# Relative-position attention before a dense block: the softmax reciprocals of a head pair leave for DRAM in three transfers instead of sixteen

## The chip, the core and the metric

One NeuronCore of a Trainium2 chip runs the whole kernel. The metric is the device time of one execution in microseconds (us), lower is better; a kernel's figure is the median of its timed runs. The profile is of one more execution, taken by the hardware profiler.

## What is computed

Attention for 8 batch elements, 8 heads, 576 positions and a head width of 64, with a bias that a small two-layer network makes from the distance of two positions, and then a dense block on the 4608 tokens. Cut to what matters:

```python
scores = q @ k.T / sqrt(64) + bias[h]            # 576 x 576 for each batch element and head
attn   = exp(scores - max(scores, axis=-1))
attn   = attn / (sum(attn, axis=-1) + 1e-09)     # the sums this change is about
x      = (attn @ v), heads side by side          # 4608 tokens x 512
out    = ((x @ w1) * (x @ w2)) @ w3 @ w_out
```

The kernel leaves the division for later: it stores the unnormalised product `exp(...) @ v` and, apart from it, the reciprocals of the sums, and multiplies the two when the dense block loads its tokens.

## The kernel before

**Stages.** A first stage (to about 60 us of the trace) makes the bias. Then come 32 attention units of about 12.2 us each, up to about 470 us: unit u is head pair p = u // 8 and batch element b = u % 8 (`units`). The dense block fills the rest, and TensorE (PE) is busy there without a break that matters here.

**One unit.** Nine tiles of scores (`TILES`, "0" to "7" for four row blocks of each of two heads, "M" for the last 64 rows of both heads) go through `op_S` (PE), `op_T` (VectorE, DVE: bias and row maximum), `op_E` (ScalarE, ACT: exponential, with the row sum as a by-product), `op_F` (PE transposes), `op_H` (ACT or DVE move them out of PSUM) and `op_W` (PE: times v). The steps of consecutive units overlap. On PE, ACT, DVE and GpSimd (POOL) the order is written out by hand in `ORDER`, one start time per step in a unit of `PERIOD`, and each engine executes in that order: an instruction that waits holds all behind it. The order of the DMA issues on the SP queue isn't written out; the Tile scheduler decides it. The SP queue, too, is worked off in order.

**The sums.** `sums[p]` is one tile of 128 x 72: a column for each tile of each of the eight units of a head pair. In the last unit of a pair `op_r` adds 1e-9 and takes the reciprocal (L529, L530), `op_F` "N" transposes the 72 columns, `op_H` "N" copies them to `rts[p]` (72 x 128), and `op_r` "d" writes `rts[p]` to `r_d` in DRAM, laid out head by head and there token by token (L534, L535): two DMAs for each of the eight batch elements. This happens four times, after units 7, 15, 23 and 31. The readers of `r_d` are the loads of the dense block (`load_x`, L836), which begin after unit 31.

**A piece of a weight in each unit.** The dense block's weights arrive in 8-byte form and are turned to float32 in pieces, one in most units (`pieces`; none in units 7, 8, 15, 23 and 31). The eight steps of a piece come from `narrow`: `fetch` (L322, a load of 512 KB into `wi` on the SP queue), `size` (L327, ACT), `rest` (L333, POOL), `clamp`, `shift`, `head` and `power` (DVE, `power` at L359) and `total` (L364 and L365, POOL). There is one buffer `wi` for all pieces, so a `fetch` waits until the piece before has done L364, the last step that reads it. The steps have their places in `ORDER` as "c1" to "c7"; "c1" (L327) stands between two exponentials of ACT.

**Other loads on the SP queue.** In each unit `load` issues `rq` and `rk` (L452, the unit's q and k), `rv` (L452) and `rt` (L456, the last 64 columns of q), and `op_x` stores the product (L608).

Of the kernel before, what the change touches and what calls it, by code (L numbers as in the profile page):

```python
# [13 lines left out]
AF = mybir.ActivationFunctionType  # L14
# [4 lines left out]
P = 128  # L19
# [239 lines left out]
def relpos_attention_moe(  # L259
# [17 lines left out]
    nc = tc.nc  # L277
    NPAIR, B, _, S = k.shape
# [120 lines left out]
    r_d = [r_all[:, p] for p in range(NPAIR)]  # L399
# [13 lines left out]
    NB, sums, rts = {}, {}, {}  # L413
# [5 lines left out]
    def halves(x):  # L419
        return x.rearrange("p (a j) -> p a j", a=2)  # L420
# [90 lines left out]
    def op_E(u, t):  # L511
        d = st[u]
        ts, mx = d.pop(("t", t))
        p, b = units[u]
        if p not in sums:
            sums[p] = sm.tile([P, 9 * B], F32, name="sum")
        if t == "M":
            pp, col = PM2[u % 2][:, 64:64 + S], 8
        else:
            h, i = int(t) % 2, int(t) // 2  # L520
            if ("P", i) not in d:
                d["P", i] = ppool.tile([P, 2 * S], F32, name="pp", bufs=NPP)
            pp, col = d["P", i][:, h * S:(h + 1) * S], i + 4 * h
        nc.scalar.activation(pp, ts, AF.Exp, bias=mx, scale=-1.0, accum_out=sums[p][:, 9 * b + col:9 * b + col + 1])  # L524

    def op_r(u, n):
        p, b = units[u]
        if n == "":
            nc.vector.tensor_scalar(sums[p], sums[p], 1e-9, None, op0=ALU.add)  # L529
            nc.vector.reciprocal(sums[p], sums[p])  # L530
        else:
            for c in range(B):
                rows, x = r_d[p][:, c * S:(c + 1) * S], rts[p][9 * c:9 * c + 9]
                nc.sync.dma_start(rows[:, 0:512].rearrange("h (i j) -> h i j", j=P), x[0:8])  # L534
                nc.sync.dma_start(rows[:, 512:S].rearrange("(o h) j -> o h j", o=1), x[8:9])  # L535

    def turn(ps, c0, x):
        for hf, rows in enumerate((lo, hi)):
# [80 lines left out]
    for m, u in enumerate(UP_IN):  # L619
        w = (moe_w1, moe_w2)[m].rearrange("(c p) n -> p c n", p=P)[:, :, 0:P]  # L620
        x = wu0[:, (1 - m) * DM:(2 - m) * DM]
        pieces[u] = narrow(cva, w, DM, x, nc.sync, pieces=NC, low=nc.gpsimd, both=True)

    def op_c(u, n):
        pieces[u][int(n)]()

    made = dict(l=lambda u, n: load(u, n[1]), g=op_g, S=op_S, T=op_T, E=op_E, r=op_r, F=op_F, W=op_W, x=op_x, c=op_c)
    later = []
    for (n, u), (at, on) in arrange(NU, pieces).items():
# [112 lines left out]
    PM2 = [ppool.tile([P, S + P], F32, name=f"ppM{i}") for i in range(2)]  # L742
# [556 lines left out]
    for c in range(NPR):  # L1299
# [8 lines left out]
        if c + 1 < NPR:  # L1308
            x = next(coming)
# [9 lines left out]
        if prior:  # L1319
            e, d = prior[-1], down["1"]  # L1320
# [5 lines left out]
        d = down["4"]  # L1326
# [76 lines left out]
```

## Time and profile before

| | |
|---|---|
| median of 3 runs | 1069.78 us (1069.55 to 1073.88) |
| profiled execution, its own time | 1068.68 us |
| its span (first to last instruction) | 1066.5 us |
| mean granted clock of PE | 0.988 |
| PE, DVE, ACT, POOL busy | 97%, 77%, 62%, 34% of the span |
| DMA issues `r_d<-rt` on the SP queue | 32 of 4 KB (L534), 32 of 0.5 KB (L535) |

The profiled execution lies 2.2 us over its span and 1.1 us under the median. Times of the trace count from the start of the span. "SPq" names an issue on the SP queue: its duration is how long the queue is held, not how long the data travel. A note in brackets behind an instruction is the idle time of its engine before it and what ended that. A granted clock of 1.00 is PE's upper level (2.4 GHz), 0.50 the lower (1.2 GHz).

### The profile page before, as it was taken

What the parts mean: (1) busy time and instruction counts of PE and PEld (TensorE: products, weight loads), DVE (VectorE), ACT (ScalarE), POOL (GpSimd) and SP (SyncE); (2) the same over time, 40 slices, a digit from 0 to 9 for tenths busy, and PEclk for the clock granted to TensorE, in tenths of its full rate; (3) what the DMA queues carried; (4) which work ended last, traced back from release to release, by engine and by line L of the source; (5) the groups of instructions that cost most, each with busy time, mean ns of one, the idle gap of its engine ahead of it and who ended that gap; (6) DMA issues with size and microseconds to landing.
All of it is one profiled execution on the core that took longest, in us unless ns stands there. A gap on an engine that the chain in (4) does not pass through costs nothing. (4 is left out here: it accounts for less than half of the span.)

```text
span 1066.5 us, 22676 instructions
## 1 busy us (share of the span) xinstructions
PE 1029.6 (97%) x8816; PEld 826.0 (77%) x8816; DVE 818.9 (77%) x1529; ACT 658.5 (62%) x1199; POOL 360.1 (34%) x337
## 2 busy tenths in 40 slices
PE   6979999999799979999999999999999999999998
PEld 2357777777577757767899998888888888888887
DVE  8968888888588868856988997978477757774664
ACT  8879989998599969973644553445234533453232
POOL 0067755675567656722000154611211111100100
PEclk9989999999899989999999999999999999999999
DMA  7965474547454645316569669885777577743623
GB/s 244 312 185 172 155 252 142 189 155 233 141 167 158 211 146 165 122 64 162 169 211 307 255 236 334 284 281 183 225 247 268 185 230 242 271 150 122 234 96 136
DMA packets 80331, 214.39 MB, mean 201 GB/s; under 512 B 11232, under 2 KB 29024, under 8 KB 75104
## 3 DMA queue, kind: packets, MB, share of 16 engines
q1 hardware_dynamic: 66080, 142.30, 41.1%
q0 software_dynamic: 13136, 68.98, 19.7%
q10 hardware_dynamic: 1008, 1.66, 0.5%
q8 instruction: 70, 1.15, 0.4%
q14 instruction: 37, 0.30, 0.1%
HBM read 163.06 MB, written 49.84 MB: 200 GB/s over the span
## 5 line engine op out<-in xcount | busy, mean ns | idle before, releaser
L1092 PE MATMUL b<-xu,w 128*128 128x462 f32 (+1 forms) x1728 | 366.2, 372 | 1.1 <-ACT wos L1103 0.9
L1092 PEld LDWEIGHTS b<-xu,w 128*128 128x128 f32 x1728 | 325.2, 188 | 38.7 <-ACT wos L1103 1.3
L499 DVE CUSTOM_DVE_ANT_0 ts<-s,nb 128x576 f32<-128x576 f32 x288 | 208.1, 754 | 42.3 <-ACT pp L524 16.8
L524 ACT ACTIVATE pp<-ts,mx 128x576 f32<-128x576 f32 x256 | 195.4, 766 | 4.4 <-DVE mx L499 4.4
L1092 PE MATMUL b<-xu,w3s 128*128 128x462 f32 (+1 forms) x840 | 179.6, 372 | 0.0
L1092 PEld LDWEIGHTS b<-xu,w3s 128*128 128x128 f32 x840 | 158.1, 188 | 18.0
L599 PE MATMUL pst<-pt,rv 128*64 128x256 f32 (+1 forms) x1280 | 171.9, 416 | 0.2 <-ACT pt L567 0.2
L1103 ACT COPY wos<-b 128x462 f32<-128x462 f32 (+1 forms) x151 | 81.2, 542 | 137.5 <-PE b L1092 135.6
L930 DVE TENSOR_TENSOR wos<-b,wos 128x462 f32<-128x462 f32 (+1 forms) x126 | 79.7, 637 | 111.5 <-PE b L1092 109.9
L567 ACT ACTIVATE pt<-pst 128x1024 f32<-128x1024 f32 x128 | 130.4, 1021 | 42.7 <-PE pst L540 42.1
L599 PEld LDWEIGHTS pst<-pt,rv 128*64 128x64 f32 x1280 | 87.2, 138 | 63.6 <-issue 8.1
L565 DVE COPY pt<-pst 64x64 f32<-64x64 f32 (+3 forms) x160 | 82.2, 514 | 40.0 <-PE pst L599 35.2
L540 PE MATMUL pst<-ident,pp 64*128 64x64 f32 x2304 | 95.8, 225 | 12.7 <-ACT pt L567 12.1
L540 PEld LDWEIGHTS pst<-ident,pp 64*128 64x128 f32 x2304 | 90.2, 141 | 14.0 <-ACT pt L567 12.9
L488 PE MATMUL s<-kh,qh 64*128 64x288 f32 x512 | 96.3, 367 | 4.8 <-POOL kh L470 3.1
L850 ACT ACTIVATE w<-wu 128x768 fp32r<-128x768 f32 (+1 forms) x45 | 40.4, 907 | 95.8 <-PE b L1092 73.3
L1084 POOL DMA_DIRECT2D w<-ws_d x24 | 17.3, 721 | 202.3 <-PE b L1092 186.0
L850 ACT ACTIVATE xu<-g 128x924 fp32r<-128x924 f32 (+1 forms) x60 | 55.9, 969 | 41.4 <-DVE g L930 39.7
L1278 POOL DMA_DIRECT2D w3s<-dw_d x33 | 18.0, 547 | 181.3 <-DVE w3s L853 111.7
L488 PE MATMUL s<-kh,ql 64*128 64x288 f32 x512 | 78.0, 298 | 0.6 <-DVE ql L468 0.6
L488 PE MATMUL s<-kl,qh 64*128 64x288 f32 x512 | 77.8, 297 | 0.7 <-POOL kl L471 0.7
L471 POOL TENSOR_TENSOR ql<-rq,qh 128x1024 fp32r<-128x1024 f32 x31 | 73.9, 2385 | 2.6
(118 smaller groups left out, 1464.4 us busy)
## 6 DMA issues: line engine op xcount, KB each, us to landing
w3s<-dw_d POOLq DMA_DIRECT2D x33, 1024.0 KB, 7.2
w<-ws_d POOLq DMA_DIRECT2D x24, 1024.0 KB, 5.6
rq<-in_q_dram SPq DMA_DIRECT2D x28, 512.0 KB
wi<-in_moe_w_dram SPq DMA_DIRECT2D x22, 512.0 KB
nb_d<-bev SPq DMA_DIRECT2D x36, 295.5 KB
rv<-in_v_dram SPq DMA_DIRECT2D x32, 320.0 KB
x_d<-pt SPq DMA_DIRECT2D x32, 288.0 KB
wu<-wu_d SPq DMA_DIRECT2D x24, 384.0 KB
```

The costliest lines, as they stand in the source:

```text
L471: nc.gpsimd.tensor_tensor(l, x, f(h), op=ALU.subtract)
L488: nc.tensor.matmul(s[:, hf, :HS], Q[x][rows, h * 512 + i * P:h * 512 + (i + 1) * P], K[y][rows, h * HS:(h + 1) * HS], start=(m == 0), stop ...
L499: nc.vector.tensor_tensor_reduce(out=halves(ts), in0=d.pop(("s", t))[:, :, :HS], in1=halves(NB[p, t]), op0=ALU.add, op1=ALU.min, scale=-1. ...
L524: nc.scalar.activation(pp, ts, AF.Exp, bias=mx, scale=-1.0, accum_out=sums[p][:, 9 * b + col:9 * b + col + 1])
L540: nc.tensor.transpose(ps[0:n, hf, c0:c0 + 64], x[rows], ident[rows, rows])
L565: nc.vector.tensor_copy(o, x)
L567: nc.scalar.activation(o, x, AF.Copy)
L599: nc.tensor.matmul(o, x[:, c0:c0 + D], m, start=(c == 0), stop=(c == 4))
L850: nc.scalar.activation(o, x, AF.Copy)
L930: return lambda: nc.vector.tensor_tensor(o(), a(), b(), op=op)
L1092: nc.tensor.matmul(acc, w(l), x(r), start=start and i == 0, stop=stop and i == 2, skip_group_check=True)
L1103: return h, pl.step("ACT", 0.16 + n / 1200, lambda: nc.scalar.copy(spare(h, n)(), bank(src, n)()), after, [src], [h])
```

## The change

The 72 columns of `sums[p]` get another order. Before, unit b owned columns 9b to 9b+8: four of head 0, four of head 1, one of tile M. Now head 0 has columns 0 to 31, head 1 columns 32 to 63 (4b + i within the head), and tile M of all units columns 64 to 71. After the transpose these columns are rows of `rts[p]`, so that all of a head's rows stand together in the order in which `r_d` wants them. The write to DRAM is then one DMA of 32 x 128 for each head and one of 8 x 128 for the M rows, in place of eight DMAs of 8 x 128 and eight of 1 x 128. The bytes, and the runs of 512 and 256 bytes that they are made of, are the same. The exponential, the addition, the reciprocal, the transposes and the copy keep their sizes.

```diff
--- before.py
+++ after.py
@@ -515,13 +515,13 @@
         if p not in sums:
             sums[p] = sm.tile([P, 9 * B], F32, name="sum")
         if t == "M":
-            pp, col = PM2[u % 2][:, 64:64 + S], 8
+            pp, col = PM2[u % 2][:, 64:64 + S], 8 * B + b
         else:
             h, i = int(t) % 2, int(t) // 2
             if ("P", i) not in d:
                 d["P", i] = ppool.tile([P, 2 * S], F32, name="pp", bufs=NPP)
-            pp, col = d["P", i][:, h * S:(h + 1) * S], i + 4 * h
-        nc.scalar.activation(pp, ts, AF.Exp, bias=mx, scale=-1.0, accum_out=sums[p][:, 9 * b + col:9 * b + col + 1])
+            pp, col = d["P", i][:, h * S:(h + 1) * S], 4 * (h * B + b) + i
+        nc.scalar.activation(pp, ts, AF.Exp, bias=mx, scale=-1.0, accum_out=sums[p][:, col:col + 1])
 
     def op_r(u, n):
         p, b = units[u]
@@ -529,10 +529,13 @@
             nc.vector.tensor_scalar(sums[p], sums[p], 1e-9, None, op0=ALU.add)
             nc.vector.reciprocal(sums[p], sums[p])
         else:
-            for c in range(B):
-                rows, x = r_d[p][:, c * S:(c + 1) * S], rts[p][9 * c:9 * c + 9]
-                nc.sync.dma_start(rows[:, 0:512].rearrange("h (i j) -> h i j", j=P), x[0:8])
-                nc.sync.dma_start(rows[:, 512:S].rearrange("(o h) j -> o h j", o=1), x[8:9])
+            x = rts[p]
+            rows = r_d[p].rearrange("h (c j) -> h c j", j=S)
+            for h in range(2):
+                nc.sync.dma_start(
+                    rows[h][:, 0:512].rearrange("c (i j) -> c i j", j=P), x[4 * B * h:4 * B * (h + 1)],
+                )
+            nc.sync.dma_start(rows[:, :, 512:S].rearrange("h c j -> c h j"), halves(x[8 * B:9 * B]))
 
     def turn(ps, c0, x):
         for hf, rows in enumerate((lo, hi)):
```

On PE, ACT, DVE and POOL the instructions stand in the same order as before. On the SP queue only the sixteen transfers of each head pair are replaced. `DMAHW` names one of eight counters which the DMAs of the hardware queues use in turn; a wait on one is a wait for the DMA that used it last.

The SP queue after unit 15 (head pair 1), before. Ahead stands the load of k, behind the transfers the load of the last q columns (L456), the piece of unit 17 (L322) and a later unit's q (L452):

```order
L452 DMA rk<-in_k_dram 128x576 [waits DMAHW4_49,PE_49]
L534 DMA r_d<-rt 2x4x128 [waits DMAHW5_49,DVE_49]
L535 DMA r_d<-rt 2x1x64 [waits DMAHW6_49]
...
L534 DMA r_d<-rt 2x4x128 [waits DMAHW3_49]
L535 DMA r_d<-rt 2x1x64 [waits DMAHW4_49]
L456 DMA rt<-in_q_dram 128x128 [waits DMAHW5_49]
L322 DMA wi<-in_moe_w_dram 128x1024 [waits DMAHW6_49,Activation_49,Pool_49]
L452 DMA rq<-in_q_dram 128x1024 [waits DMAHW7_49,Pool_49]
```

The same place now:

```order
L452 DMA rk<-in_k_dram 128x576 [waits DMAHW7_49,PE_49]
L535 DMA r_d<-rt 8x4x128 [waits DMAHW0_49,DVE_49]
L535 DMA r_d<-rt 8x4x128 [waits DMAHW1_49]
L538 DMA r_d<-rt 8x2x64 [waits DMAHW2_49]
L456 DMA rt<-in_q_dram 128x128 [waits DMAHW3_49]
L322 DMA wi<-in_moe_w_dram 128x1024 [waits DMAHW4_49,Activation_49,Pool_49]
L452 DMA rq<-in_q_dram 128x1024 [waits DMAHW5_49,Pool_49]
```

Thirteen issues between the load of k and the load of `rt` are gone, and the piece's load keeps its place behind `rt`; it waits as before for ACT and POOL, the readers of the piece before. Units 23 to 25 (head pair 2) read the same.

The SP queue after unit 7 (head pair 0), before; no piece stands right behind the transfers here, since the load for unit 9 was issued far ahead:

```order
L452 DMA rk<-in_k_dram 128x576 [waits DMAHW7_49,PE_49]
L534 DMA r_d<-rt 2x4x128 [waits DMAHW0_49,DVE_49]
...
L535 DMA r_d<-rt 2x1x64 [waits DMAHW7_49]
L456 DMA rt<-in_q_dram 128x128 [waits DMAHW0_49]
L452 DMA rq<-in_q_dram 128x1024 [waits DMAHW1_49,Pool_49]
L452 DMA rv<-in_v_dram 128x640 [waits DMAHW2_49,PE_49]
```

The same place now:

```order
L452 DMA rk<-in_k_dram 128x576 [waits DMAHW7_49,PE_49]
L535 DMA r_d<-rt 8x4x128 [waits DMAHW0_49,DVE_49]
L535 DMA r_d<-rt 8x4x128 [waits DMAHW1_49]
L538 DMA r_d<-rt 8x2x64 [waits DMAHW2_49]
L456 DMA rt<-in_q_dram 128x128 [waits DMAHW3_49]
L452 DMA rq<-in_q_dram 128x1024 [waits DMAHW4_49,Pool_49]
L452 DMA rv<-in_v_dram 128x640 [waits DMAHW5_49,PE_49]
```

Here, too, thirteen issues are gone, ahead of `rt`, `rq` and `rv`.

## Rows read from the trace of the kernel before

**Rows 1.** The page, part 1: busy time, share of the span, instructions of each engine

```profile
PE 1029.6 (97%) x8816; PEld 826.0 (77%) x8816; DVE 818.9 (77%) x1529; ACT 658.5 (62%) x1199; POOL 360.1 (34%) x337
```

**Rows 2.** Waits of PE, whole span: us in total, times, longest

```profile
PE pst L540 <- ACT pt L567: 12.1, 3, 6.2
```

**Rows 3.** Timeline of PE: start us, us, line, operation, [idle before it <- releaser]

```profile
183.62 0.27 PE L547 MATMUL pst<-ident,ppM 64*128 64x64 f32 x1
...
195.85 0.27 PE L547 MATMUL pst<-ident,ppM 64*128 64x64 f32 x1
...
269.61 0.27 PE L547 MATMUL pst<-ident,ppM 64*128 64x64 f32 x1
...
278.04 1.11 PE L540 MATMUL pst<-ident,pp 64*128 64x64 f32 x16 [6.18 <-ACT pt L567]
...
290.82 0.27 PE L547 MATMUL pst<-ident,ppM 64*128 64x64 f32 x1
...
376.74 0.27 PE L547 MATMUL pst<-ident,ppM 64*128 64x64 f32 x1
...
384.64 1.12 PE L540 MATMUL pst<-ident,pp 64*128 64x64 f32 x16 [5.66 <-ACT pt L567]
...
397.05 0.27 PE L547 MATMUL pst<-ident,ppM 64*128 64x64 f32 x1
```

**Rows 4.** Stretches: busy us (instructions) by engine, PEclk granted, DMA share, GB/s

```profile
core 0: us, PE busy (x) PEld busy (x) DVE busy (x) ACT busy (x) POOL busy (x), PEclk, DMA share, GB/s
181.00:193.00 12.00, 12.00 (x180) 8.75 (x178) 10.41 (x28) 11.11 (x24) 8.54 (x8) 1.00 0.55 170
266.00:278.00 12.00, 5.85 (x84) 4.04 (x82) 5.70 (x17) 4.98 (x12) 5.18 (x5) 0.95 0.55 173
278.00:290.00 12.00, 11.96 (x124) 8.26 (x124) 7.67 (x18) 9.03 (x19) 8.70 (x7) 0.76 0.32 95
...
465.00:471.00 6.00, 4.57 (x54) 2.78 (x50) 3.98 (x5) 5.27 (x11) 2.55 (x2) 1.00 0.14 45
```

**Rows 5.** Waits of ACT, 60 to 470 us: us in total, times, longest

```profile
ACT wmag L327 <- DMA wi<-in_moe_w_dram: 13.5, 2, 7.0
```

**Rows 6.** Timeline of ACT: the first step of the pieces of units 11, 17, 25

```profile
194.02 0.69 ACT L327 ACTIVATE wmag<-wi 128x512 f32<-128x512 f32 x1
...
274.90 0.66 ACT L327 ACTIVATE wmag<-wi 128x512 f32<-128x512 f32 x1 [7.02 <-DMA wi<-in_moe_w_dram]
...
381.50 0.66 ACT L327 ACTIVATE wmag<-wi 128x512 f32<-128x512 f32 x1 [6.51 <-DMA wi<-in_moe_w_dram]
```

**Rows 7.** Timeline of the SP queue: pieces (L322) and transfers of head pair 1

```profile
189.93 0.33 SPq L322 DMA_DIRECT2D wi<-in_moe_w_dram  x1
...
258.82 0.63 SPq L534 DMA_DIRECT2D r_d<-rt  x1
...
268.43 0.55 SPq L535 DMA_DIRECT2D r_d<-rt  x1
...
269.55 0.35 SPq L322 DMA_DIRECT2D wi<-in_moe_w_dram  x1
...
376.27 0.67 SPq L322 DMA_DIRECT2D wi<-in_moe_w_dram  x1
...
487.84 0.38 SPq L322 DMA_DIRECT2D wi<-in_moe_w_dram  x1
```

**Rows 8.** Timeline of POOL: the step that frees the landing buffer, units 10, 16, 24

```profile
188.61 1.29 POOL L364 TENSOR_TENSOR wos<-wos,wi 128x512 f32<-128x512 f32 x1 [3.06 <-DVE wi L359]
...
262.40 1.28 POOL L364 TENSOR_TENSOR wu<-wu,wi 128x512 f32<-128x512 f32 x1 [5.92 <-DVE wi L359]
...
369.37 1.29 POOL L364 TENSOR_TENSOR wu<-wu,wi 128x512 f32<-128x512 f32 x1 [3.97 <-DVE wi L359]
```

**Rows 9.** Other issues on the SP queue, by line: duration ns min/median/max, first and last start

```profile
L456 SPq DMA_DIRECT2D rt<-in_q_dram x32: 328/481/1432, 2.1 to 434.5; - x32
...
L720 SPq DMA_DIRECT2D nb_d<-bev x36: 517/568/1674, 10.3 to 55.4; - x36
```

## The prediction

> **What bounds the kernel now.** The page's busy times come first: PE is busy for 1029.6 of 1066.5 us [rows 1], so only what puts PE back to work sooner can shorten the run by much. The waits of PE come next: the longest entry is 12.1 us in three waits of the transposes (L540) for a move by ACT, one of them 6.2 us [rows 2]. The timeline of PE shows where: 6.18 us before 278.04 and 5.66 us before 384.64 [rows 3]. To see what such a place costs in all, take the distance between the "N" transposes (L547) of consecutive units. In an undisturbed unit it is 195.85 - 183.62 = 12.23 us. Up to unit 17 it is 290.82 - 269.61 = 21.21, up to unit 25 it is 397.05 - 376.74 = 20.31 [rows 3]. The losses are 8.98 and 8.08 us, **17.06 us together**. They are more than the idle time, 11.84 us, since PE works slowly after it: the granted clock was 1.00 between 181 and 193 us, but 0.76 between 278 and 290, part of it at the lower level, 1.2 GHz [rows 4]. The slow work thus costs 8.98 - 6.18 = 2.80 and 8.08 - 5.66 = 2.42 us.
>
> What does ACT wait for? Its waits in the attention stage name the piece's load `wi`: 13.5 us in two waits [rows 5]; they stand before L327 at 274.90 (7.02 us) and 381.50 (6.51 us) [rows 6]. ACT works in order, so the exponentials and moves behind L327 stood too. The load of the first was issued at 269.55, after sixteen transfers that held the queue from 258.82 on; that of the second at 376.27 [rows 7]. ACT was free for L327 at 274.90 - 7.02 = 267.88, before the load was even issued.
>
> **The change part by part.** *The queue.* From the first of the sixteen transfers (258.82) to the last (268.43) there are 15 steps of 0.64 us; the last and the load of `rt` behind it take another 1.12 us, to 269.55 [rows 7]. With three transfers in place of sixteen, 13 x 0.64 = 8.33 us go, and the queue would come to the piece's load at 261.22. It can't be issued then: it waits for L364 of unit 16 on POOL, which starts at 262.40 [rows 8]. In unit 10 the load followed the start of L364 by 189.93 - 188.61 = 1.32 us [rows 7, 8], so here it goes out at 263.72, 5.83 us earlier than before. For unit 25 the queue comes to it at 376.27 - 8.33 = 367.94, POOL allows it at 369.37 + 1.32 = 370.69, 5.58 us earlier. The transfers themselves are then hidden behind POOL's step, with 2.5 and 2.75 us to spare.
>
> *Whether this is early enough.* The piece that was issued at 189.93 was read by ACT at 194.02 with no wait noted, 4.09 us later [rows 6, 7]; and the two waits above are all that ACT has for a piece [rows 5]. Unit 17 now has 267.88 - 263.72 = 4.16 us and unit 25 has 374.99 - 370.69 = 4.30, both more than 4.09. Behind the load the queue is as it is in an undisturbed unit, too, since the next load of q has to wait for POOL. So I take it that nothing of the two waits is left, that the two units become ordinary ones, and with the idle time the fall of the clock goes. What is late next is PE itself, at 12.23 us a unit.
>
> *Price of a new transfer.* The trace has none of 32 x 128 to DRAM; I bound it by other issues on the same queue. Loads of 128 x 128 (L456) held it for 0.33 at the least and 0.48 us at the median; the three-dimensional stores of the bias (L720) for 0.57 at the median and 1.67 at the most [rows 9]. I take the 0.64 of the old transfers, as the nearest in shape, and to DRAM as well. At 0.33 each nothing is won beyond this, since POOL sets the issue. At 1.67 each, with 1.12 - 0.64 = 0.48 for `rt`, the load goes out at 258.82 + 5.01 + 0.48 = 264.31, 0.59 late. For unit 25 the first transfer starts at about 376.27 - 9.61 - 1.12 = 365.54 by the same spacing, so the load goes out at 371.03, 0.34 late.
>
> *Travel of the load.* In the two bad places it took up to 274.90 - 269.55 = 5.35 and 381.50 - 376.27 = 5.23 us to arrive [rows 6, 7], with the loads of q, v and k right behind it. At these figures ACT would still wait 5.35 - 4.16 = 1.19 and 0.93 us. Of the old waits PE felt 7.02 - 6.18 = 0.84 and 0.85 us less than ACT, so it would idle 0.35 and 0.08 us. With the late issue that is at most 0.94 and 0.42, 1.4 us in all. I take zero, the undisturbed unit being the nearest row, and keep 1.4 for the range. Short gaps need not lower the clock: between 465 and 471 us PE was busy for only 4.57 of 6 us and the clock stayed at 1.00 [rows 4].
>
> *The other two places.* After unit 7 no piece stands behind the transfers, and ACT has no wait for one there [rows 5]: zero, covered because that piece was fetched far ahead. After unit 31 the next piece's load goes out at 487.84 [rows 7], and the sixteen, at 0.64 each, would hold the queue no longer there than the 10.7 us of unit 15; PE has other work by then, and the list of its waits has nothing bigger than the row quoted [rows 2]: zero. The columns' new order leaves every instruction of ACT, DVE and PE at its size: zero.
>
> **The sum.** The profiled execution took 1068.68 us; 1068.68 - 8.98 - 8.08 = 1051.6. It lay 1.1 us under the median of the runs shown, 1069.78; on that base the forecast is 1069.78 - 17.06 = **1052.7 us**.
>
> *A rule against it.* The sixteen small transfers held the queue for 10.3 us, about twice as long as the piece's load then took to arrive (5.35) [rows 6, 7]. The Trainium skill ("DMA: Bandwidth & Descriptors", section "Issuing engines are not separate DMA queues") says that the time which a sequencer needs to start a DMA is usually small beside the DMA itself. By that rule the place of the load in the queue would hardly matter and the time would stay at 1069.8; here the rows speak for the exception.
>
> **The rivals.** (1) *The load still comes late, and the clock falls again.* It issues early, but travels 5.3 us, and the short stall that is left is enough to lower PE's clock in both units. Kept are 0.35 + 0.08 of idle time and 2.80 + 2.42 of slow work, 5.65 us: 1058.4. For it: the travel times as measured. Against it: the loads that crowded it then are held back now, and PE kept its clock in the gaps after 465 us.
> (2) *The change doesn't do what it says, because an issue costs by its rows.* An old transfer of 8 x 128 has 8 runs of 128 and a new one 32, so it would hold the queue 4 x 0.64 = 2.56 us; the last has 16 runs instead of 2, 8 x 0.64 = 5.12. Together 10.24, as much as the sixteen: 1069.7, no change. Against it: 128 x 128 held the queue for 0.48 us [rows 9].
> (3) *The issue isn't what is late, the travel is* (the mechanism behind the rule above): the load would arrive when it did however early it goes out, 1069.8. Against it: 4.09 us sufficed in unit 11.
> (4) *Slower: the three transfers hold the queue longer than sixteen did.* This decides from 10.3 / 3 = 3.4 us each. At 4.4 each the load in both units goes out 2.9 us later than before, PE stands 5.8 us longer in all: 1075.6. Against it: nothing among the rows of this queue that I use goes beyond 1.67 [rows 9].
>
> **How the numbers follow.** Forecast 0.87; rival (1) 0.06; (2) 0.03; (3) 0.02; (4) 0.02. A measurement of this kernel can tell about 0.5%, 5.3 us, from no change. Faster by more: 0.87 + 0.06 = 0.93. Within: 0.03 + 0.02 = 0.05. Slower: 0.02. The range covers the forecast alone, which is enough for 8 in 10. Its upper end is 1052.7 + 1.4 for the bounds of issue and travel + 1.1, the distance of the profiled run from the median: 1055.2. Its lower end is 1052.7 - 1.1 - 1.1, for a median that lies as low as the profiled run or lower by as much again, since no row lets more than the 17.06 be won: 1050.5.
>
> **What would show it.** In the trace after: three issues of `r_d` of about 0.6 us each per head pair; the pieces of units 17 and 25 issued within about 1.4 us of L364's start on POOL, some 5 us after the first of the three; no wait of ACT for `wi` in the attention stage; PE's wait for ACT's move down from 12.1 to under 1 us; 12.2 to 12.7 us between the N transposes of units 16 and 17, and 24 and 25; the clock at 1.00 there; the attention stage over some 17 us sooner and the dense block as long as before. I am wrong on the queue if the three take more than 5 us together, on the travel if ACT still waits for `wi`, and on the clock if a stretch under 1.00 is left without an idle stretch before it.

## The result and the profile after

The changed kernel took **1053.64 us** (median of 4 runs, 1053.17 to 1057.68) against 1069.66 us (4 runs, 1069.35 to 1073.88): ratio 0.985, 95% interval 0.9815 to 0.9884. The forecast was 1052.7 us, with a range of 1050.5 to 1055.2. The profiled execution took 1053.82 us, its span is 1051.7 us.

The page, part 1, and the waits of PE over the attention stage (60 to 470 us), as in [rows 1, 2]; the code has moved down by three lines, so L540, L567 and L547 of before are L543, L570 and L550 here:

```profile
PE 1027.7 (98%) x8816; PEld 824.3 (78%) x8816; DVE 818.9 (78%) x1529; ACT 659.0 (63%) x1199; POOL 359.9 (34%) x337
```

```profile
PE s L488 <- POOL kh L470: 4.5, 1, 4.5
PE s L488 <- DVE mx L499: 0.9, 1, 0.9
PE pst L543 <- ACT pt L570: 0.8, 3, 0.3
```

The wait that led before, 12.1 us, is down to 0.8. The SP queue around head pairs 1 and 2, as in [rows 7] (start us, held us, line, what; x2 stands for two issues in a row; L535 and L538 are the new transfers):

```profile
260.85 1.43 SPq L535 DMA_DIRECT2D r_d<-rt  x2
262.33 0.47 SPq L538 DMA_DIRECT2D r_d<-rt  x1
262.84 0.33 SPq L456 DMA_DIRECT2D rt<-in_q_dram  x1
265.22 0.33 SPq L322 DMA_DIRECT2D wi<-in_moe_w_dram  x1
...
358.98 1.44 SPq L535 DMA_DIRECT2D r_d<-rt  x2
360.46 0.46 SPq L538 DMA_DIRECT2D r_d<-rt  x1
360.97 0.33 SPq L456 DMA_DIRECT2D rt<-in_q_dram  x1
363.76 0.33 SPq L322 DMA_DIRECT2D wi<-in_moe_w_dram  x1
```

The queue is through with the transfers and the load of `rt` at 263.17, then stands idle until 265.22. What it waits for is on POOL, as in [rows 8], and the reader of the load is on ACT, as in [rows 6]; first POOL's two rows, then ACT's:

```profile
263.92 1.28 POOL L364 TENSOR_TENSOR wu<-wu,wi 128x512 f32<-128x512 f32 x1 [4.89 <-DVE wi L359]
...
362.45 1.28 POOL L364 TENSOR_TENSOR wu<-wu,wi 128x512 f32<-128x512 f32 x1 [4.51 <-DVE wi L359]
```

```profile
269.46 0.70 ACT L327 ACTIVATE wmag<-wi 128x512 f32<-128x512 f32 x1
...
367.96 0.68 ACT L327 ACTIVATE wmag<-wi 128x512 f32<-128x512 f32 x1
```

Neither of ACT's rows has a bracket: no idle time ahead of them, where 7.02 and 6.51 us stood before. How the whole span divides is best seen in stretches cut at the N transposes of units 0, 16, 17, 24, 25 and 31 (the starts of L547 or L550). Columns: stretch, its length, busy us (instructions) of PE, PEld, DVE, ACT, POOL, granted clock, DMA share, GB/s. Before:

```profile
60.00:72.47 12.47, 8.79 (x79) 6.11 (x79) 6.39 (x17) 7.14 (x14) 9.56 (x10) 0.59 0.57 160
72.47:269.61 197.14, 196.68 (x2856) 142.81 (x2852) 168.31 (x426) 178.66 (x364) 128.69 (x102) 1.00 0.56 180
269.61:290.82 21.21, 15.03 (x182) 10.49 (x178) 10.87 (x27) 12.95 (x27) 11.43 (x10) 0.84 0.48 151
290.82:376.74 85.92, 85.83 (x1253) 62.32 (x1250) 73.62 (x188) 77.16 (x157) 55.28 (x43) 1.00 0.54 173
376.74:397.05 20.31, 14.65 (x183) 10.37 (x180) 10.87 (x27) 12.98 (x27) 11.43 (x10) 0.83 0.50 156
397.05:473.15 76.10, 74.23 (x1046) 53.26 (x1042) 61.07 (x151) 67.38 (x136) 40.14 (x32) 1.00 0.41 132
```

After:

```profile
60.00:74.19 14.19, 8.85 (x78) 6.11 (x78) 7.03 (x17) 7.19 (x15) 11.21 (x11) 0.52 0.56 152
74.19:271.28 197.09, 196.46 (x2856) 142.56 (x2852) 167.52 (x426) 180.44 (x368) 129.80 (x104) 1.00 0.57 183
271.28:283.52 12.24, 12.24 (x182) 8.91 (x178) 10.66 (x27) 11.38 (x24) 8.63 (x8) 1.00 0.52 170
283.52:369.80 86.28, 86.00 (x1253) 62.37 (x1250) 73.81 (x188) 78.81 (x161) 58.15 (x47) 1.00 0.58 186
369.80:382.02 12.22, 12.22 (x183) 8.88 (x180) 10.65 (x27) 11.24 (x24) 8.63 (x8) 1.00 0.51 167
382.02:458.14 76.12, 74.26 (x1046) 53.27 (x1043) 61.08 (x151) 67.60 (x136) 41.99 (x34) 1.00 0.43 138
```

All of the gain stands in the third and the fifth row: 21.21 - 12.24 = 8.97 us and 20.31 - 12.22 = 8.09 us, 17.06 together. In both, PE does its 182 or 183 matmuls without a gap and at the upper clock; its busy time there falls by 2.79 + 2.43 = 5.22 us with no matmul less (granted clock 0.84 and 0.83 before, 1.00 now), which is the clock's part. Elsewhere the profiled execution lost a little: 1.72 us ahead of unit 0, 0.36 in the fourth stretch, and from the last N transposes to the end 593.56 us against 593.35. The span is thus 17.06 - 1.72 - 0.36 - 0.21 + 0.03 (the other two stretches) = 14.80 us shorter.

### The profile page after: what moved, and what is told of

Its sections match the earlier page's. It is cut to its first block, busy times and chain, and to the rows that moved or that the text cites. A ratio compares the mean times of both kernels' runs of the same rounds, so it can differ in the third digit from the quotient of the medians.

```text
span 1051.7 us, 22621 instructions
## 1 busy us (share of the span) xinstructions
PE 1027.7 (98%) x8816; PEld 824.3 (78%) x8816; DVE 818.9 (78%) x1529; ACT 659.0 (63%) x1199; POOL 359.9 (34%) x337
## 5 line engine op out<-in xcount | busy, mean ns | idle before, releaser
L602 PE MATMUL pst<-pt,rv 128*64 128x256 f32 (+1 forms) x1280 | 169.3, 411 | 0.2 <-ACT pt L570 0.2
L570 ACT ACTIVATE pt<-pst 128x1024 f32<-128x1024 f32 x128 | 130.5, 1021 | 37.2 <-PE pst L543 36.5
L543 PE MATMUL pst<-ident,pp 64*128 64x64 f32 x2304 | 95.0, 224 | 1.4 <-ACT pt L570 0.8
L543 PEld LDWEIGHTS pst<-ident,pp 64*128 64x128 f32 x2304 | 89.3, 140 | 2.9 <-ACT pt L570 1.6
```

The lines of the kernel that those rows point to most:

```text
L543: nc.tensor.transpose(ps[0:n, hf, c0:c0 + 64], x[rows], ident[rows, rows])
L570: nc.scalar.activation(o, x, AF.Copy)
L602: nc.tensor.matmul(o, x[:, c0:c0 + D], m, start=(c == 0), stop=(c == 4))
```

## The experiments

The theory: the load of a weight piece (the expectations also say expert piece) stands behind the transfers on an in-order queue; only how long these hold the queue past POOL's release matters, and only where such a load stands behind them. The main rivals: the gain comes from fewer transfers in general (each costs something wherever it stands), or the travel and not the issue was late. All in one table, with PE's distance between the N transposes of units 16 and 17, and of 24 and 25 (12.2 us undisturbed):

| kernel | transfers per head pair | 16 to 17 | 24 to 25 | ratio to before (95%) |
|---|---|---|---|---|
| pairs12 | 3 in pairs 1 and 2, else 16 | 12.25 | 12.21 | 0.9855 (0.9832 to 0.9879) |
| pairs03 | 3 in pairs 0 and 3, else 16 | 20.90 | 20.52 | 0.9992 (0.9976 to 1.0007) |
| groups2 | 6 | 12.25 | 12.22 | 0.9843 (0.9819 to 0.9867) |
| groups4 | 12 | 15.78 | 14.13 | 0.9907 (0.9885 to 0.9928) |
| groups8 | 24 | 23.21 | 23.52 | 1.0045 (1.0023 to 1.0066) |
| before_early | 16, pieces a unit earlier | 12.23 | 12.24 | 0.9843 (0.9815 to 0.9871) |
| after_early | 3, pieces a unit earlier | 12.24 | 12.23 | 0.9837 (0.9814 to 0.9861) |
| after_again | 3 | 12.24 | 12.23 | 0.9861 (0.9839 to 0.9883) |
| before_again | 16 | 20.49 | 20.64 | 0.9993 (0.9984 to 1.0002) |
| after_third | 3 | 12.25 | 12.22 | 0.9845 (0.9832 to 0.9859) |
| before_early_b | 16, pieces a unit earlier | 12.23 | 12.23 | 0.9848 (0.9834 to 0.9861) |
| after_early_b | 3, pieces a unit earlier | 12.23 | 12.22 | 0.9850 (0.9836 to 0.9863) |

They were timed in three groups, each on one chip beside the kernel before. That took 1068.71 us beside pairs12, pairs03, groups4 and before_early, 1073.09 us beside groups2, groups8, after_again and after_early, and 1069.64 us beside the last four. So the ratios can be compared over the whole table, and medians only within a group; the expectations name times that go by the 1069.7 us of the result.

### The change in two of its four places

**pairs12**: the new columns and the three transfers only for the head pairs with a piece behind them; the other two keep the old code.

```diff
...
-            pp, col = d["P", i][:, h * S:(h + 1) * S], 4 * (h * B + b) + i
+            pp, col = d["P", i][:, h * S:(h + 1) * S], 4 * (h * B + b) + i if p in (1, 2) else 9 * b + i + 4 * h
...
-            x = rts[p]
-            rows = r_d[p].rearrange("h (c j) -> h c j", j=S)
...
+            if p in (1, 2):
+                x = rts[p]
...
+            else:
+                for c in range(B):
...
```

> New columns and three transfers for head pairs 1 and 2 alone; pairs 0 and 3 keep the old columns and sixteen transfers. Theory (only the piece loads of units 17 and 25, which stand behind the transfers of pairs 1 and 2, matter): the whole gain, 1053.6 us, no wait of ACT for wi at units 17 and 25. Rival A (any time freed on the SP queue is worth the same): half the gain, about 1061.6 us. Rival B (the gain lies in the fewer transfers before the dense block): none, 1069.7 us.

Measured: 1053.55 us, ratio 0.9855. The whole gain is there.

**pairs03** has the same edit with `if p in (0, 3)`, the two places where the prediction put the worth at zero.

> The mirror image: new columns and three transfers for head pairs 0 and 3 alone, pairs 1 and 2 as before the change. Theory: no gain, 1069.7 us, ACT waits 6.5 to 7 us for wi at units 17 and 25 and PE stands about 6 us at each. Rival A: about 1061.6 us. Rival B: 1053.6 us.

Measured: 1068.93 us, ratio 0.9992. Waits of PE and of ACT, 60 to 470 us:

```profile
PE pst L549 <- ACT pt L576: 11.5, 3, 5.7
...
ACT wmag L327 <- DMA wi<-in_moe_w_dram: 12.9, 2, 6.6
```

They read like [rows 2, 5]. Of the 52 issues that the change saves, the 26 in these places are worth nothing that can be measured (the interval leaves room for a gain of 2.6 us at most). So in this kernel the place of an issue has a price, and the issue by itself none that shows.

### How many transfers are few enough

Three kernels cut each of the three new transfers into 2, 4 or 8 along the batch, with the columns as in the changed kernel (here 4):

```diff
-            for h in range(2):
-                nc.sync.dma_start(
-                    rows[h][:, 0:512].rearrange("c (i j) -> c i j", j=P), x[4 * B * h:4 * B * (h + 1)],
-                )
-            nc.sync.dma_start(rows[:, :, 512:S].rearrange("h c j -> c h j"), halves(x[8 * B:9 * B]))
+            n = B // 4
+            for c in range(0, B, n):
+                for h in range(2):
+                    nc.sync.dma_start(
+                        rows[h][c:c + n, 0:512].rearrange("c (i j) -> c i j", j=P), x[4 * B * h + 4 * c:4 * B * h + 4 * (c + n)],
+                    )
+                nc.sync.dma_start(rows[:, c:c + n, 512:S].rearrange("h c j -> c h j"), halves(x[8 * B + c:8 * B + c + n]))
```

> The new columns, each of the three transfers cut in two: six issues for a head pair. In the kernel with the change the three of pair 1 held the queue for 2.0 us and POOL let the piece's load go 4.4 us after the first; six hold it for about 3.7 us, and 0.5 us for rt. Theory (POOL's step hides the issues until they take more than that): units 17 and 25 within 0.2 us of 12.24 us, whole kernel 1053.6 us, give or take 1.5 us for the start. Rival (every issue costs its own time): three more of 0.55 us in two places, 3.3 us more, 1057 us.

> The new columns, but each of the three transfers cut in four along the batch elements: twelve issues for a head pair. At 0.64 us each they hold the queue for 7.7 us, and with 0.5 us for rt the piece's load goes out 3.3 us after POOL allows it (before the change: 5.8 and 5.6). Theory: ACT waits 3.3 to 4.5 us at units 17 and 25 and PE idles 2.4 to 3.6 us at each; if PE's clock holds, 1058.5 to 1061 us, if it falls as before (2.4 to 2.8 us each), up to 1066 us. Rival C (the order of the columns itself is what helps, not the count of issues): 1053.6 us.

> The new columns, each transfer cut in eight: 24 issues for a head pair, more than the 16 before the change. With 0.56 us an issue, as in the kernel with twelve, they hold the queue for 13.5 us; with 0.64 us 15.4 us. The piece's load then goes out 3.2 to 5.1 us later than with sixteen. Theory: units 17 and 25 lose 12 to 14 us each instead of 9.0 and 8.1, whole kernel 1077 to 1082 us, slower than before the change. Rival C (the columns' order helps by itself): not slower than 1069 us.

Measured: 1055.27 us for groups2, 1059.17 for groups4, 1077.15 for groups8 (ratios in the table). The first lies 0.2 us above its range, with both units within 0.02 us of 12.24.

Six transfers (groups2) cost as little as three: they hold the queue from 261.43 to 265.10, 3.67 us, and the piece's load then waits for POOL until 266.32 all the same. Twelve (groups4) no longer fit. The SP queue's last rows, ACT's reader and PE behind it, in unit 16 to 17:

```profile
268.26 0.36 SPq L456 DMA_DIRECT2D rt<-in_q_dram  x1
268.74 0.36 SPq L322 DMA_DIRECT2D wi<-in_moe_w_dram  x1
...
273.22 0.67 ACT L327 ACTIVATE wmag<-wi 128x512 f32<-128x512 f32 x1 [2.79 <-DMA wi<-in_moe_w_dram]
...
276.37 1.12 PE L545 MATMUL pst<-ident,pp 64*128 64x64 f32 x16 [1.97 <-ACT pt L572]
```

Twenty-four (groups8) are slower than the kernel before, though with the new order of columns: the first starts at 260.18, the load goes out at 272.29, and

```profile
278.14 0.66 ACT L327 ACTIVATE wmag<-wi 128x512 f32<-128x512 f32 x1 [8.88 <-DMA wi<-in_moe_w_dram]
...
281.28 1.12 PE L545 MATMUL pst<-ident,pp 64*128 64x64 f32 x16 [8.05 <-ACT pt L572]
```

The chain can be followed in numbers. POOL allows the load 1.32 us after L364 starts, which is 4.9 us after the first transfer in before and the three groups, and 4.4 us in the changed kernel (groups8: L364 at 263.76, so 265.08). "Late" is how long after that the load goes out:

| unit 16 to 17 of | late | ACT waits | PE idle | PE loses in all | of it slow work |
|---|---|---|---|---|---|
| after, groups2 | 0 | 0 | 0 | 0 | 0 |
| groups4 | 2.49 | 2.79 | 1.97 | 3.55 | 1.58 |
| before | 5.83 | 7.02 | 6.18 | 8.98 | 2.80 |
| groups8 | 7.21 | 8.88 | 8.05 | 10.98 | 2.93 |

ACT comes free for L327 some 4.2 us after POOL's release, and the three loads that were late took 4.48, 5.35 and 5.85 us from their issue to L327. So ACT's wait is the lateness and what the travel took beyond 4.2 us; PE idles some 0.8 us less than ACT waits, and the clock adds the rest.

Two forecasts missed by size, both because the queue was held for less time than assumed. The twelve transfers of groups4 cost (268.26 - 261.34) / 12 = 0.58 us each and not 0.64, so the load was 2.49 us late and not 3.3, and ACT's and PE's waits lie under their forecasts in both units; the median lies in its range all the same. In groups8 the queue was to be held for 13.5 to 15.4 us and was held for 11.6, 0.48 us for an issue; the units lose 10.98 and 11.29 us and not 12 to 14, and by the ratio the kernel is some 5 us slower than before where at least 7 was forecast. The price doesn't go by the bytes alone: in groups8 a head's transfer of 4 x 128 held the queue for 0.38 us (two in 0.76, as most of its rows read), and the M transfer, a quarter of that size, for 0.57.

### The other remedy: leave the transfers, move the pieces

**before_early** keeps the sixteen transfers and works the pieces of units 16 and 24 one unit earlier. The landing buffer then comes free a unit earlier too, and the next loads, those of units 17 and 25, stand ahead of the transfers on the queue:

```diff
-UP_IN = 16, 24
+UP_IN = 15, 23
```

> The kernel before with its sixteen transfers; the two pieces of moe_w1 and moe_w2 are worked in units 15 and 23 in place of 16 and 24, so that the loads of units 17 and 25 are issued ahead of the sixteen transfers, as that of unit 9 is. Theory (what hurts is that this load stands behind the transfers): the gain without any change to them, 1053 to 1055 us, no wait of ACT for wi at units 17 and 25. Rival D (ten us of issues in a row on the queue delay something else just as much, once the piece is out of the way): 1060 us or more, with a new wait behind the transfers.

Measured: 1050.88 us, ratio 0.9843, some 2 us better than the range. In the trace of its SP queue the piece's load and the first and last of the same sixteen transfers:

```profile
252.32 0.37 SPq L322 DMA_DIRECT2D wi<-in_moe_w_dram  x1
...
258.09 0.63 SPq L534 DMA_DIRECT2D r_d<-rt  x1
...
268.79 0.55 SPq L535 DMA_DIRECT2D r_d<-rt  x1
269.39 0.40 SPq L456 DMA_DIRECT2D rt<-in_q_dram  x1
```

The burst is as long as ever (258.09 to 269.39), and unit 17 follows 16 after 12.23 us. ACT has no wait for `wi` in units 17 and 25. So it isn't the burst that costs, nor its bytes, but what stands behind it.

**after_early** makes the same edit in the changed kernel, and so has both remedies.

> Both at once: three transfers, and the pieces of units 16 and 24 moved to units 15 and 23, so that the loads of units 17 and 25 also go out ahead of the transfers. Theory (each alone removes the same wait): no further gain in units 17 and 25, within 0.5 us of the better of the two, 1050.5 to 1053.5 us. If the two gains were of different waits they would add up, some 15 us less, 1038 us.

Measured: 1055.40 us, ratio 0.9837: no more than either alone. The time lies above the range named, beside a kernel before that took 1073.09 us. The gains don't add, as they are the same wait.

### Once more, side by side

**after_again** is the changed kernel a second time, beside groups2 and groups8.

> The kernel with the change once more, unaltered, for its ratio on the same chip as the other runs and for a second profile. Theory: units 17 and 25 at 12.2 to 12.3 us; the first N transpose anywhere between 71.9 and 74.9 us, since the kernels so far, which are alike up to there, spread over that; median 1052 to 1054 us. If the 1.7 us by which the start came later in the first profile belonged to the change, it would be at 74 us again.

Measured: 1057.75 us, ratio 0.9861; the time lies above the 1052 to 1054 us named, again beside 1073.09. The two units were as they should be, and unit 0's N transposes started at 73.91 us. But from the last N transposes to the end its profiled execution took 597.2 us and that of after_early 597.1, where the changed kernel's first took 593.56. In after_again POOL's four subtractions for one tile took 11.14 us, and PE then stood 3.6 us (timeline of POOL, then the waits of PE from 480 us on):

```profile
594.31 11.14 POOL L1076 TENSOR_TENSOR wu<-wu 128x256 f32<-128x256 f32 x4 [6.53 <-DVE w L856]
605.39 1.62 POOL L1281 DMA_DIRECT2D w3s<-dw_d  x3
```

```profile
PE b L1095 <- DMA w3s<-dw_d: 3.6, 1, 3.6
```

Both had three transfers, and groups2 and groups8 on the same chip hadn't shown it, so it could have been a late price of the change. Four kernels side by side were to tell: before, changed, and each with the pieces a unit earlier.

> The kernel before, unchanged, so that the four kernels of this call have a profile each from one chip. If the theory holds (the transposes of the probabilities for units 17 and 25 of the attention wait because the expert pieces stand behind sixteen DMA issues on SP's queue), the interval from the N transposes of unit 16 to those of unit 17 is about 21.2 us and that of units 24 to 25 about 20.3 us, against 12.2 undisturbed, and the time is that of the kernel before, ratio 1.000. On the dense block after the attention: two earlier profiles of kernels with three transfers showed POOL's four subtractions for one tile taking 11.1 us instead of 6.2 and TensorE then waiting 3.5 us for a weight load. If that belongs to the run or the chip, it may stand in this profile too, and the stretch from the last N transposes to the end is about 597 us; if it belongs to the three transfers, the stretch is 593.3 us here.

> The changed kernel. Theory: intervals at units 17 and 25 of 12.2 us each, 17.1 us less than before in sum, ratio 0.984 to 0.987. Dense block: 593.3 us from the last N transposes to the end if the longer stretch of the two earlier profiles was of the run; 597 us if it belongs to three transfers in place of sixteen (then it costs the change some 3.7 us of its gain, and the time would be that much nearer to the kernel before).

> Sixteen transfers, with the two expert pieces one unit earlier, so that their loads are issued ahead of the transfers. Theory: no stall at units 17 and 25, 12.2 us each, and the ratio of the changed kernel within 0.3% (0.983 to 0.987). If the longer dense block belongs to the three transfers, this kernel has the 593.3 us stretch and is faster than the changed kernel by up to 3.7 us (0.35%); if it belongs to the run or the chip, the two agree within 2 us.

> Both: three transfers and the pieces one unit earlier. Theory: the two remedies take away the same wait, so the gains don't add: 12.2 us at units 17 and 25, and a time within 2 us of either alone; it is the best of the four only by the 1 us waits of ScalarE for expert pieces that three transfers alone still showed in two units. If the two gains added, it would be some 17 us faster than the changed kernel, near 1036 us.

Measured: 1069.15, 1053.29, 1053.17 and 1053.45 us (ratios in the table). From the last N transposes to the end it is 593.31, 593.47, 593.34 and 593.73 us, and in after_third the same four subtractions read

```profile
592.31 6.22 POOL L1076 TENSOR_TENSOR wu<-wu 128x256 f32<-128x256 f32 x4 [6.52 <-DVE w L856]
```

So the longer dense block belongs to those two profiled executions and not to the three transfers; why POOL took longer there stays open. In before_again the two units lose as before, 20.49 and 20.64 us long. The three kernels without the stall lie within 0.3 us of each other: there is no version among these that beats the changed one by anything that could be measured, and moving the pieces would have given the same with two numbers.

## Why the prediction was right

**The bound.** The loss was put at 8.98 + 8.08 us in two units. In the windows above the same stretches shrink by 8.97 and 8.09, split as forecast: 11.84 us of idle time, and 5.22 us less busy time for the same matmuls, part of which had run at the lower clock.

**The queue.** A new transfer was to cost about 0.64 us; 32 x 128 took 0.64 to 0.78 (two in 1.43 us) and the M rows 0.30 to 0.47. From the first of the three to the `rt` behind them it is 1.99 us. Rival (2), by which a transfer costs by its rows and the three 10.2 us, is out; so is rival (4), which needed 3.4 us each. The load was to go out 1.32 us after L364 starts; it did after 1.30 and 1.31, with 2.05 and 2.46 us to spare (forecast: 2.5 and 2.75). That this cover is real, and where it ends, is what the groups show: six transfers fit under it, twelve don't.

**The travel.** The two loads were read after 4.24 and 4.20 us with no wait, so neither the 1.4 us kept for the range nor rival (1) was needed; what rival (1) says of a short stall and the clock did happen in groups4, where 1.97 us of idle time was followed by 1.58 us of slow work. Rival (3), by which the load arrives when it does however early it goes out, is refuted twice, by the change and by before_early. The rule that was weighed (the Trainium skill, "DMA: Bandwidth & Descriptors", section "Issuing engines are not separate DMA queues": starting a DMA usually takes little beside the DMA) doesn't carry here, where starts add up: sixteen held the queue longer than the piece's load behind them travelled, and from six on the ratio follows the number of starts behind which that load stands, at equal bytes.

**What was mis-sized.** I took it that ACT would wait for no piece. It did, in two units that the change doesn't touch; in units 4 and 21; these are ACT's waits for `wi`, 60 to 470 us of the changed kernel, and the place in unit 21:

```profile
ACT wmag L327 <- DMA wi<-in_moe_w_out_dram: 1.1, 1, 1.1
ACT wmag L327 <- DMA wi<-in_moe_w_dram: 1.0, 1, 1.0
```

```profile
319.44 0.70 ACT L327 ACTIVATE wmag<-wi 128x512 f32<-128x512 f32 x1 [0.99 <-DMA wi<-in_moe_w_dram]
```

This load went out at 314.28 and took 5.16 us. The 4.09 us on which I relied is no travel time: the written order brings ACT to L327 some 4.1 us after most issues, so a read without a wait says only that the load was there by then. There is hardly any slack, and a slow load shows. In unit 21 it cost PE 12.66 - 12.22 = 0.44 us. On the SP queue no load of q, v or k followed it closely (the next issue was at 319.13), so the crowding by those loads, which the prediction held against rival (1), isn't needed for a slow load. The wait in unit 4 stands ahead of the first new transfer (162.3 us). Such waits also come and go between executions of one kernel (after_again has none in unit 21), and kernels with sixteen transfers show them (pairs03 0.52 us in unit 4, before_early_b 1.60 us in unit 18, where PE lost 1.00 us). So nothing ties them to the change; what makes these loads slow isn't shown. I was lucky that they fell where they did: a 5.3 us load in unit 17 would have used up about 1 us of ACT's time.

**The sum.** 17.06 us was forecast and won in the two units; 16.0 by the medians (1069.66 - 1053.64), 14.86 by the two profiled executions, whose attention stage ends 15.0 us sooner and not some 17. The largest part missing from the latter is ahead of unit 0, where PE waited 4.53 us for the rounded k that POOL makes instead of 3.06 (before, then after):

```profile
61.76 0.59 PE L488 MATMUL s<-kh,qh 64*128 64x288 f32 x2 [3.06 <-POOL kh L470]
...
63.34 0.61 PE L488 MATMUL s<-kh,qh 64*128 64x288 f32 x2 [4.53 <-POOL kh L470]
```

Nothing of the change has run by then. Over the fourteen profiles unit 0's N transposes start between 71.92 and 74.89 us, with sixteen transfers (71.92 to 73.47) and with three (72.30 to 74.19) alike. This is the spread that the range had room for.

**The other two places** were put at zero; pairs03 measures 0.9992 (0.9976 to 1.0007) for them.

## What to carry to other kernels

On an in-order DMA queue a burst of small issues is priced by what stands behind it. Find the first load after the burst whose reader is waiting, work out when its buffer would let it go anyway, and count only the time beyond that: below this point fewer issues win nothing more (six were as good as three), and moving the one load ahead of the burst wins the same as making the burst short. Add to the wait what PE's clock costs after it, here up to 3.2 us a wait.

## What the runs showed of the hardware

Whether PE's clock falls in a short gap was close here. In groups4 nearly the same gap stands in two units: 1.97 us of idle time ahead of 276.37, shown above, and 1.68 us ahead of 378.83. PE's row of the second, then windows of 2 us, two for the first gap and one for the second, columns as above:

```profile
378.83 0.71 PE L545 MATMUL pst<-ident,pp 64*128 64x64 f32 x16 [1.68 <-ACT pt L572]
```

```profile
276.00:278.00 2.00, 1.63 (x22) 1.63 (x24) 1.83 (x6) 2.00 (x5) 0.11 (x1) 0.53 0.61 225
278.00:280.00 2.00, 2.00 (x16) 1.26 (x14) 1.75 (x5) 2.00 (x5) 1.57 (x2) 0.61 0.11 43
...
379.00:381.00 2.00, 2.00 (x34) 1.58 (x34) 1.83 (x5) 2.00 (x4) 0.20 (x1) 1.00 0.46 169
```

After the first the clock was at the lower level for most of 4 us and the unit lost 3.55 us; after the second it stayed at 1.00 and the unit lost 1.90. Whether the 0.29 us between them or something else decided isn't shown.

The slow work after a long gap isn't of one size either. Over the eight long gaps (5.51 to 8.61 us, two each in before, before_again, pairs03 and groups8) it cost 1.56 to 3.16 us, and not more where the gap was longer. It goes with how long the clock stays down after PE has started again. The extremes are unit 24 to 25 of before_again and unit 16 to 17 of pairs03; PE's row, then windows of 1 us in which the clock falls and rises, first before_again, then pairs03:

```profile
386.29 1.12 PE L540 MATMUL pst<-ident,pp 64*128 64x64 f32 x16 [6.85 <-ACT pt L567]
...
278.87 1.12 PE L549 MATMUL pst<-ident,pp 64*128 64x64 f32 x16 [5.51 <-ACT pt L576]
```

```profile
382.00:383.00 1.00, 0.00 (x0) 0.00 (x0) 0.00 (x0) 0.00 (x0) 0.00 (x0) 0.81 0.95 373
389.00:390.00 1.00, 1.00 (x7) 0.46 (x9) 0.86 (x4) 1.00 (x3) 0.92 (x2) 0.78 0.00 0
...
278.00:279.00 1.00, 0.13 (x2) 0.13 (x4) 1.00 (x3) 1.00 (x2) 0.62 (x1) 0.70 0.61 206
285.00:286.00 1.00, 1.00 (x8) 0.28 (x4) 0.00 (x0) 0.00 (x0) 1.00 (x1) 0.89 0.12 49
```

By these shares the clock fell at about 382.6 and rose at about 389.4 in the first, and at 278.4 and 285.2 in the second. PE thus worked at half the speed for 3.2 us in the first, for 6.3 in the second, and lost about half of that: 1.6 and 3.2 us, against 20.64 - 6.85 - 12.23 = 1.56 and 20.90 - 5.51 - 12.23 = 3.16 measured. In the first the clock fell 3.2 us after PE had stopped, in the second 5.0 us, so in the first more of the low stretch passed while PE stood anyway.
